# One attention tile for the last 64 queries of both heads, inverse sums written 64-fold, and a plan with new ranks, waits and banks

## The chip, the cores and the metric

The kernel runs on one core of one Trainium2 chip. The metric is the device time of one execution in microseconds (us), the median over several runs. The core's engines work side by side, each on its own queue of instructions in a fixed order, and wait for one another by semaphores: TensorE (PE), VectorE (DVE), ScalarE (ACT), GpSimd (POOL) and SyncE (SP), which here issues the DMA transfers.

## What is computed

Attention with a rotary embedding over 2 batches, 8 heads, 576 positions and 64 channels, then a gated two-layer block without nonlinearity, then eight experts whose weights come from eight rounds of row and column normalisation. The change touches the first part and one product of the second:

```
scores = scale * q_rot @ k_rot.T
scores = scores - max(scores, axis=-1)
attn   = exp(scores)
attn   = attn / (sum(attn, axis=-1) + 1e-09)
x      = attn @ v                       # (1152, 512) after the heads are joined
h      = (x @ w1) * (x @ w2) @ w3
y      = h @ w_out                      # the kernel forms w3 @ w_out first
out    = sum over e of P[:, e] * (relu(y @ moe2_w1[e]) @ moe2_w2[e])
```

## The kernel before

Every float32 product outside the attention weights is split into a high and a low part and made from two or three matmuls. The program has three stages: attention (with the product of w3 and w_out, called w34, beside it), the gated block (`branch`, `merge`), and the experts (`hidden`, `project`). The change lies in the first.

**Tiles.** Two heads form a pair; there are 8 pairs (`NP`). A pair has 576 queries a head, in five query tiles of 128 (`NQ`). The fifth holds 64 queries and 64 columns of zeros (`SPAD` is 640). For each query tile i and head j of pair n: `scores` (L304) makes 128 x 576 scores in PSUM on PE, `row_max` (L329) finds the negated row maximum on DVE, `exponentials` (L333) writes the exponentials and their row sums `sm` on ACT, `transposes` (L348) turns them on PE in three parts a query tile, `moved` (L355) copies each part from PSUM to `et` on ACT or DVE. The tiles form two groups a pair (`TILES`: tiles 0 and 1, tiles 2 to 4). For each group `norm_rows` (L361, L362) adds 1e-9 to the sums on DVE and takes their reciprocals, 4 or 6 numbers a partition; `norm_columns` (L369) spreads each over 64 rows and transposes it by a matmul against the identity; `norm_moved` (L374) copies the result to `r`; `values` (L382) multiplies by v; `x_scale` (L390) multiplies by `r`; `x_hi` and `x_lo` (L401, L405) split the result.

**Conversions.** The weights of the gated block arrive as 64-bit words. One load of 512 KB (`wide`) needs three DVE steps (L183 `low_bits`, L186 `signed`, L191 `joined`), two on ACT (L178, L196) and a subtraction `lo_part` (L199) on POOL or DVE. There are 8 such loads of w_out, 16 of w3, and in the gated block 16 of w1 and w2 (`w12_unit`).

**w34.** `w34_product(u, j)` is three matmuls of 512 columns (L226 to L228). Eight products fill one bank of PSUM, which `w34_hi` (ACT, L233) and `w34_lo` (DVE, L238) then empty. Bank i = 0 to 6 lies in the one-slot pool `psW`; bank 7 (`NEARLY`) is made after the attention stage in the pool `u` of the gated block.

**The order.** A `Plan` sets each engine's order while the program is built. It simulates the engines with a cost for each step and, whenever an engine is free, takes the ready step of lowest rank. `SIGNAL` is what a result costs on the way to another engine; `slots` are the buffers. The steps then stand in this order in the queues; on the chip each engine follows its queue whatever the real durations are. Products of w34 have rank 1000 (L524), so the plan takes one only when PE has nothing else ready. Until the first product, idle time that the plan sees on PE is filled with matmuls of the identity (L541, tile `w`). After the plan come `w12_unit(0)`, the eight products of bank 7, and the branches of the gated block (L140 to L142; their gate product `gf` on DVE is L584).

Of the kernel before, what the change touches and what calls it, by code (L numbers as in the profile page):

```python
# [18 lines left out]
P = 128  # L19
# [20 lines left out]
NEARLY = 7  # L40
NSTEP = 2 * E
# [7 lines left out]
class Plan:  # L49
# [5 lines left out]
    SIGNAL = dict(pe=0.28, act=0.12, dve=0.1, pool=0.12, sp=1.7)  # L55
# [11 lines left out]
    def order(self):  # L67
# [7 lines left out]
        def start(needs, takes, e, ports):  # L75
# [7 lines left out]
            at = [t + (0.0 if by == e else self.SIGNAL[by]) for t, by in map(done.get, needs)]  # L83
# [32 lines left out]
def attention_two_moes(ctx: ExitStack, tc: tile.TileContext, rope, qk, v, mw12, mw3t, mwo, wg, ew1, ew2, out):  # L116
# [20 lines left out]
    def three(ps, terms):  # L137
# [15 lines left out]
    psW, psX, psS, psT = (  # L153
        aps.enter_context(tc.tile_pool(name=n, bufs=k, space=PSUM)) for n, k in (("psW", 1), ("psX", 1), ("psS", 2), ("psT", 2))
# [95 lines left out]
    QK0 = [first[:, o : o + 2 * n].rearrange("p (a s) -> p a s", a=2) for o, n in ((0, SPAD), (2 * SPAD, S))]  # L250
# [52 lines left out]

    def scores(n, i, j):  # L304

        if j == 0:
            st["e", n, i] = att_p.tile([P, 2, S], F32, name="e", bufs=2)
            st["nm", n, i] = att_p.tile([P, 2], F32, name="nm", bufs=4)
            g, k, _ = group(i)
            if k == 0:  # L310
                st["sm", n, g] = att_p.tile([P, 3, 2], F32, name="sm", bufs=3)
        js = half(j)
        if n:
            q, k = SQ[n % 2][:, j], keys(n)
            terms = [(q, k[:, j]), (q, k[:, 2 + j])]
        else:
            (qh, ql), (kh, kl) = ([t[js, x] for x in range(2)] for t in QK0)
            terms = [(qh, kh), (qh, kl), (ql, kh)]
        st["s", n, i, j] = ps = psS.tile([P, 2, 512], F32, name="s")
        for x, (q, k) in enumerate(terms):  # L320
            for h in range(2):
                pe.matmul(  # L322
                    ps[:, h, :HS], q[:, i * P : (i + 1) * P], k[:, h * HS : (h + 1) * HS],
                    start=(x == 0), stop=(x == len(terms) - 1),
                )
# [5 lines left out]
    def exponentials(n, i, j):  # L331
# [3 lines left out]
            AF.Exp, bias=st["nm", n, i][:, j : j + 1], accum_out=st["sm", n, g][:, k, j : j + 1],  # L335
        )

    def transposes(n, i, part):

        rows = min(P, S - i * P)  # L340
        e = st["e", n, i].rearrange("p j r -> p (j r)")
# [589 lines left out]
```

## Time and profile before

| | us |
|---|---|
| median of 3 runs | 1174.78 |
| lowest, highest | 1173.91, 1178.76 |
| the profiled execution | 1180.39 |
| its span | 1178.6 |
| PE busy | 1148.2 (97% of the span) |
| DVE busy | 730.7 (62%) |
| ACT busy | 427.7 (36%) |

The profiled execution is 5.6 us above the median; its rows are used for durations and differences. The shares are means over three stages. The attention stage ends at 212.3 us, the first matmul of the gated block starts at 246.05 us, and from 300 us on PE is busy throughout. In a view by stretches, "busy" counts time in which at least one instruction of the engine is under way; PE's matmuls overlap, so a PE that is busy all the time can still be far from its best rate.

### The profile page before, as it was taken

To read this page: it belongs to the slowest core of one execution; us is meant where nothing else is said; L and a number is where in the kernel's file an instruction comes from. 1 tells how busy PE (TensorE), PEld (TensorE's weight loads), DVE (VectorE), ACT (ScalarE), POOL (GpSimd) and SP (SyncE) were. 2 spreads that over 40 slices of the span, in tenths; PEclk is the share of its full clock that TensorE was granted. 3 is DMA by queue.
4 is the path that set the end of the run, shared out by engine and by line. 5 is a ranking of instruction groups with operands and counts; after the bars stand their busy time and mean duration, and the time that the engine had idled before them with its cause. 6 is when DMAs were issued, how large, how long until landed. Compare 5 with 4: busy or idle time off the path is not lost.

```text
span 1178.6 us, 17761 instructions
## 1 busy us (share of the span) xinstructions
PE 1148.2 (97%) x7087; PEld 1009.4 (86%) x7087; DVE 730.7 (62%) x1347; ACT 427.7 (36%) x903; POOL 203.7 (17%) x205
## 2 busy tenths in 40 slices
PE   8989999889999999999999999999999999999998
PEld 7666677688999888889898898998988989889887
DVE  5788777686443485656566556565565666565643
ACT  3767577344332342323232223223222232222311
POOL 2456451142000000201201011111020120110100
PEclk7999999999999999999999999999999999999999
DMA  6766562343100011211111111111021111110102
GB/s 216 199 182 192 168 181 75 105 148 108 54 19 18 19 37 36 71 37 37 54 36 55 36 36 56 53 36 54 20 71 37 36 55 51 40 54 19 36 9 72
DMA packets 28034, 83.07 MB, mean 70 GB/s; under 512 B 3760, under 2 KB 5296, under 8 KB 27952
## 3 DMA queue, kind: packets, MB, share of 16 engines
q1 hardware_dynamic: 27408, 81.36, 22.1%
q8 instruction: 55, 0.90, 0.3%
q10 hardware_dynamic: 544, 0.59, 0.2%
q14 instruction: 27, 0.22, 0.1%
HBM read 67.19 MB, written 2.36 MB: 59 GB/s over the span
## 4 chain that ended last, share of the span: by engine, by line
PE 87%; DVE 7%; DMA 3%; issue 1%; ACT 1%; POOL 0%; SPq 0%; ACTq 0%; DVEq 0%
PE z L764 11%; PE z L763 11%; PE z L765 11%; PE T L722 4%; PE T L723 4%; PE T L724 4%; PE s L322 3%; PE x L382 3%; PE t L348 3%; PE Q L724 3%; PE Q L722 3%; PE Q L723 3%; PE A L724 3%; PE A L723 3%; PE A L722 3%; PE u L140 3%
## 5 line engine op out<-in xcount | busy, mean ns | idle before, releaser
L765 PE MATMUL z<-w,h 128*128 128x512 f32 x576 | 226.3, 393 | 0.0
L772 DVE SCALAR_TENSOR_TENSOR acc<-z,pr,acc 128x512 f32<-128x512 f32 x135 | 101.0, 748 | 56.7 <-PE z L765 56.6
L765 PEld LDWEIGHTS z<-w,h 128*128 128x128 f32 x576 | 108.0, 187 | 25.3 <-DVE h L729 0.2
L764 PE MATMUL z<-w,y 128*128 128x512 f32 x320 | 126.4, 395 | 0.0
L763 PE MATMUL z<-w,y 128*128 128x512 f32 x320 | 126.4, 395 | 0.0
L642 POOL TENSOR_TENSOR sums<-wide 128x256 f32<-128x256 f32 x28 | 22.9, 818 | 575.3 <-DMA wide<-in_ew_dram 313.6
L764 PE MATMUL z<-w,h 128*128 128x512 f32 x256 | 101.6, 397 | 0.0
L763 PE MATMUL z<-w,h 128*128 128x512 f32 x256 | 100.8, 394 | 0.0
L134 ACT CAST w<-wide 128x768 fp32r<-128x768 f32 (+1 forms) x64 | 60.4, 943 | 93.4 <-PE z L764 65.1
L728 ACT ACTIVATE y<-tmp 128x320 fp32r<-128x320 f32 x96 | 45.2, 470 | 113.8 <-DVE tmp L744 62.3
L728 ACT ACTIVATE h<-tmp 128x256 fp32r<-128x256 f32 x96 | 39.9, 416 | 127.4 <-DVE tmp L744 120.8
L135 DVE TENSOR_TENSOR w<-wide,w 128x768 fp32r<-128x768 f32 (+1 forms) x64 | 69.6, 1088 | 26.5 <-PE T L724 14.8
L140 PE MATMUL u<-x,w 128*128 128x320 f32 (+1 forms) x256 | 76.4, 298 | 3.4 <-DVE gf L584 3.0
L142 PE MATMUL u<-x,w 128*128 128x320 f32 (+1 forms) x256 | 75.7, 296 | 0.0
L141 PE MATMUL u<-x,w 128*128 128x320 f32 (+1 forms) x256 | 75.4, 295 | 0.0
L329 DVE TENSOR_REDUCE nm<-s 128x1 f32<-128x576 f32 x80 | 59.1, 751 | 19.7 <-PE s L322 19.3
L764 PEld LDWEIGHTS z<-w,y 128*128 128x128 f32 x320 | 60.7, 190 | 5.7
L763 PEld LDWEIGHTS z<-w,y 128*128 128x128 f32 x320 | 60.2, 188 | 6.0
L333 ACT ACTIVATE e<-s,nm 128x576 f32<-128x576 f32 x80 | 59.2, 742 | 15.6 <-DVE nm L329 14.2
L729 DVE SCALAR_TENSOR_TENSOR h<-tmp,y 128x320 fp32r<-128x320 f32 x96 | 47.4, 494 | 26.0 <-ACT y L728 25.8
L348 PEld LDWEIGHTS t<-ident,e 128*128 128x128 f32 (+1 forms) x360 | 39.8, 145 | 26.0 <-ACT e L333 9.8
L722 PE MATMUL T<-x,w 128*128 128x320 f32 x192 | 60.0, 312 | 0.1
(205 smaller groups left out, 3040.5 us busy)
## 6 DMA issues: line engine op xcount, KB each, us to landing
wide<-in_ew_dram SPq DMA_DIRECT2D x64, 512.0 KB, 3.5
wide<-in_mw3t_dram SPq DMA_DIRECT2D x16, 512.0 KB, 4.1
wide<-in_mw_dram SPq DMA_DIRECT2D x16, 512.0 KB, 3.5
raw<-in_qk_dram SPq DMA_DIRECT2D x14, 576.0 KB, 4.6
kk<-raw SPq DMA_DIRECT2D x56, 144.0 KB, 3.7
wide<-in_mwo_dram SPq DMA_DIRECT2D x8, 512.0 KB, 4.3
sq<-raw SPq DMA_DIRECT2D x28, 144.0 KB, 3.4
v<-in_v_dram SPq DMA_DIRECT2D x8, 320.0 KB, 3.7
```

The costliest lines, as they stand in the source:

```text
L140: pe.matmul(ps, wh, xh, start=(i == 0), stop=False)
L141: pe.matmul(ps, wh, xl, start=False, stop=False)
L142: pe.matmul(ps, wl, xh, start=False, stop=(i == n - 1))
L348: pe.transpose(ps[:, t, :rows], e[:rows, c : c + P], ident[:rows, :rows])
L722: pe.matmul(ps, h[:, ws], x[0], start=(first and k == 0), stop=False, **kw)
L723: pe.matmul(ps, h[:, ws], x[1], start=False, stop=False, **kw)
L724: pe.matmul(ps, l[:, ws], x[0], start=False, stop=(k == 1), **kw)
L728: act.activation(h, src, AF.Relu)
L763: pe.matmul(ps, hh[:, f, ts], wh, start=(f == 0), stop=False)
L764: pe.matmul(ps, hh[:, f, ts], wl, start=False, stop=False)
L765: pe.matmul(ps, hl[:, f, ts], wh, start=False, stop=(f == FT - 1))
L772: dve.scalar_tensor_tensor(out=acc[t], in0=ps, scalar=p, in1=acc[t], op0=ALU.mult, op1=ALU.add)
```

## The change

Four query tiles of each head stay as they are. The fifth becomes one tile (`MIX`) for both heads: rows 0 to 63 are the last 64 queries of the first head, rows 64 to 127 those of the second. `mixed_scores` accumulates both heads' terms in one PSUM tile, where zeros in the other head's half keep them apart; the second head's keys stand rotated by 64 so that the nine blocks of 128 columns line up, and v is laid out to match. So a pair has 9 score tiles, row maxima and exponentials in place of 10. The query copies for the second head are split in two, so a pair has 6 of these DMAs in place of 4 (7 pairs).

The sums get their 1e-9 on ACT (`norm_sums`). `norm_rows` is now one reciprocal that reads each sum 64 times and writes 256 or 320 numbers a partition; `norm_columns` transposes that.

In the plan: products of w34 have rank 87 + 4u + j in place of 1000 + 4u + j; banks are emptied at rank -200 in place of 42; bank 6 (`LATE`) lies in the pool of the transposes; norms and values come at later ranks; L183 counts as a user of the port that DVE and POOL share; some `SIGNAL` values are larger and PE gets 0.15 more (`SLACK`); the gaps on PE are filled more fully; the PSUM pools are opened in another order.

```diff
-    SIGNAL = dict(pe=0.28, act=0.12, dve=0.1, pool=0.12, sp=1.7)
+    SIGNAL = dict(pe=0.28, act=0.14, dve=0.1, pool=0.12, sp=2.0)
+    SLACK = 0.15
...
+        dst, src = f32(SQ[n % 2][half(x ^ j), j]), raw[n, 0][half(j), 1 - x]
+        if j == 0:
+            sp.dma_start(dst[:, :S], src)
+        else:
+            sp.dma_start(dst[:, : MIX * P], src[:, : MIX * P])
+            sp.dma_start(dst[:, MIX * P + HD :], src[:, MIX * P :])
...
+    def mixed_scores(n):
+        query_tile(n, MIX)
+        st["s", n, MIX, 0] = ps = psS.tile([P, 2, 512], F32, name="s")
+        terms = []
+        for j in range(2):
...
+            pieces = [(0, 0, 0, HS), (1, 0, HS, HS)] if j == 0 else [(0, 0, HD, HS), (1, 0, HD + HS, HS - HD), (1, HS - HD, 0, HD)]
+            terms += [(q, k, pieces) for q, k in new]
...
+    def norm_sums(n, g):
+        sm = st["sm", n, g][:, : 4 + g]
+        act.activation(sm, sm, AF.Copy, bias=1e-9)
     def norm_rows(n, g):
-        dve.tensor_scalar(sm[:, :k], sm[:, :k], 1e-9, None, op0=ALU.add)
-        dve.reciprocal(sm[:, :k], sm[:, :k])
+        st["rb", n, g] = rb = att_p.tile([P, 5, D], F32, name="rb", bufs=2)
+        dve.reciprocal(rb[:, :k], sm.unsqueeze(2).to_broadcast([P, k, D]))
     def norm_columns(n, g):
-        for i in range(len(TILES[g])):
-            for j in range(2):
-                pe.matmul(ps[half(j), i], sm[:, i, j : j + 1].to_broadcast([P, D]), ident, start=True, stop=True)
+        for i in range(2):
+            pe.transpose(ps[:, i], rb[:, 2 * i : 2 * i + 2].rearrange("p j d -> p (j d)"), ident)
...
-            step(norm_rows, a, {"dve": 0.35}, r, needs)
+            step(norm_sums, a, {"act": 0.2}, r, needs)
+            step(norm_rows, a, {"dve": on_dve((4 + g) * D)}, r, [(norm_sums, *a)], [("rb", a)], [("sm", a)])
...
-            ({"dve": 0.37}, (), ["cvu"], [], ()),
+            ({"dve": 0.37}, (), ["cvu"], [], both),
...
+            bank = "psT" if i >= LATE else "psW"
+            place = (psT, "t") if i >= LATE else (psW, "w34")
-                (w34_product, u, j), {"pe": 0.7}, 1000.0 + 4 * u + j, ...
+                (w34_product, u, j), {"pe": 0.7}, 87.0 + 4 * u + j, ...
-            step(w34_hi, (i,), {"act": act_ps(DM)}, 42.0, [(w34_product, u, 3)])
+            step(w34_hi, (i,), {"act": act_ps(DM)}, -200.0, [(w34_product, u, 3)])
...
-                for _ in range(int((at - idle_from - 0.3) * 0.7 / 0.21) if filling else 0):
+                for _ in range(int((at - idle_from - 0.05) / 0.22) if filling else 0):
```

What this does to the order shows at three places. The first is PE's queue at the end of the attention stage, before: the last norm (`sm`), the last values (`x<-et`), then products of w34 (three rows each).

```order
L369 MATMUL t<-ident,sm 64x128 x6
L348 MATMUL t<-ident,e 128x64 x3
L382 MATMUL x<-et_2214,v_95 64x320 x10
L226 MATMUL w_2210<-y 128x512
L227 MATMUL w_2210<-y 128x512
L228 MATMUL w_2210<-y 128x512
L226 MATMUL w_2210<-y 128x512
L227 MATMUL w_2210<-y 128x512
L228 MATMUL w_2210<-y 128x512
```

After the last values 28 products stand here, in four banks, before bank 7 (`u`). The same place after the change:

```order
L363 MATMUL s<-kk,sq_93 128x64
L388 MATMUL t<-ident,e 128x128 x6
L391 MATMUL t<-ident,e 128x128 x4
L394 MATMUL t<-ident,e 64x64 x2
L424 MATMUL t<-ident,rb 128x128 x2
L427 MATMUL t<-ident,rb 64x64 x2
L440 MATMUL x<-et_2393,v_95 64x320 x10
L231 MATMUL u<-y 128x512
L232 MATMUL u<-y 128x512
L233 MATMUL u<-y 128x512
```

Bank 7 now follows the last values directly; the 28 products stand further up, among the attention steps of pairs 3 to 7.

The second place is such a point further up on PE, in pair 7 of the changed kernel, where one bank of w34 (`w_2028`) ends and the next (`w_2184`) begins.

```order
L231 MATMUL w_2028<-y 128x512
L232 MATMUL w_2028<-y 128x512
L233 MATMUL w_2028<-y 128x512
L391 MATMUL t<-ident,e 128x128 x4
L394 MATMUL t<-ident,e 64x64 x2
L340 MATMUL s<-kk,sq_93 128x288 x4
L440 MATMUL x<-et_1902,v_94 64x256 x2
L424 MATMUL t<-ident,rb 128x128 x2
L427 MATMUL t<-ident,rb 64x64 x2
L231 MATMUL w_2184<-y 128x512
```

A handful of attention matmuls stands between the last product of one bank and the first of the next, which waits until ACT and DVE have emptied the bank.

The third place is DVE's queue at the last group of pair 7, before:

```order
L329 TENSOR_REDUCE nm<-s 128x1 x2
L361 TENSOR_SCALAR sm<-sm 128x6
L362 RECIPROCAL sm<-sm 128x6
L355 COPY et_2214<-t 128x3x64
L199 TENSOR_TENSOR y<-cvu,y 128x512
L183 TENSOR_SCALAR cvu<-wide 128x512
L186 SCALAR_TENSOR_TENSOR cvu<-wide,cvu 128x512
L191 SCALAR_TENSOR_TENSOR cvu<-cvy,cvu 128x512
L390 TENSOR_TENSOR xs<-x,r 128x320
L405 TENSOR_TENSOR x<-xs,x 128x320
```

and after:

```order
L370 TENSOR_REDUCE nm<-s 128x1
L407 COPY et_2393<-t 128x3x128
L418 RECIPROCAL rb<-sm 128x320
L407 COPY et_2393<-t 128x3x64
L448 TENSOR_TENSOR xs<-x,r 128x320
L463 TENSOR_TENSOR x<-xs,x 128x320
L188 TENSOR_SCALAR cvu<-wide 128x512
L191 SCALAR_TENSOR_TENSOR cvu<-wide,cvu 128x512
L188 TENSOR_SCALAR cvu<-wide 128x512
L196 SCALAR_TENSOR_TENSOR cvu<-cvy,cvu 128x512
L191 SCALAR_TENSOR_TENSOR cvu<-wide,cvu 128x512
L140 TENSOR_TENSOR wgs<-wgraw,wgs 128x4x8
```

The reciprocal has 320 numbers in place of 6. Before, the conversions shown are of w3, and those of five more loads of w3 and of the two loads of `w12_unit(0)` follow the last `x_lo`. After the change the steps of w3 and of `w12_unit(0)` on DVE all stand above the last `x_lo`, and those shown below it are of `w12_unit(1)`. Ahead of the first `gf` DVE's queue holds the conversion of five w1/w2 loads in both kernels. What is left of `w12_unit(0)` stands on ACT (here the changed kernel, where `w_2498` is its tile and `w_2549` that of unit 1) and, as two `lo_part`, on POOL:

```order
L411 ACTIVATE sm<-sm 128x5
L407 COPY et_2393<-t 128x6x64
L432 COPY r<-t 128x320
L459 CAST x<-xs 128x320
L201 CAST w_2498<-cvu 128x512 x2
```

The two casts of `w_2498` come directly behind the last `x_hi`.

Counted over the plan, DVE has 72 row maxima in place of 80, 16 reciprocals of 256 or 320 numbers in place of 16 small ones with 16 additions, 4 small copies (two of 192, two of 384 numbers) in place of 7, 10 `x_lo` in place of 6 and 9 `lo_part` in place of 8; the fillers on PE are 78 in place of 49, 29 in place of 19 of them ahead of the first scores.

## Rows read from the trace of the kernel before

**Rows 1.** Stretches: length, busy us (instructions) of PE, PEld, DVE, ACT, POOL; clock; DMA.
```profile
0.00:40.00 40.00, 35.64 (x199) 29.42 (x199) 24.42 (x43) 19.23 (x42) 11.51 (x15) 0.83 0.67 205
15.00:20.00 5.00, 5.00 (x19) 4.11 (x20) 3.30 (x4) 3.17 (x7) 0.06 (x1) 0.50 0.82 286
40.00:120.00 80.00, 71.71 (x519) 52.70 (x518) 69.82 (x109) 54.79 (x131) 44.32 (x29) 0.96 0.66 193
120.00:212.30 92.30, 90.31 (x649) 64.75 (x648) 66.61 (x115) 62.59 (x151) 32.48 (x21) 0.98 0.47 133
212.30:235.20 22.90, 18.70 (x79) 14.51 (x80) 15.35 (x25) 8.89 (x16) 3.86 (x3) 1.00 0.36 119
```

**Rows 2.** Timeline of PE, 209 to 247 us: start, us, instruction [idle before <-releaser].
```profile
209.38 2.91 PE L382 MATMUL x<-et,v 128*64 128x320 f32 x20
...
216.65 0.50 PE L226 MATMUL w<-y 128*128 128x512 f32 x1 [1.40 <-DVE keep L238]
...
230.92 0.50 PE L226 MATMUL w<-y 128*128 128x512 f32 x1 [1.40 <-DVE keep L238]
...
238.85 0.50 PE L226 MATMUL u<-y 128*128 128x512 f32 x1 [2.20 <-DVE keep L238]
...
246.05 0.31 PE L140 MATMUL u<-x,w 128*128 128x320 f32 x1
```

**Rows 3.** DVE by line and shape, 0 to 246 us: busy, mean ns | idle before.
```profile
L329 DVE TENSOR_REDUCE nm<-s 128x1 f32<-128x576 f32 x80 | 59.1, 751 | 19.7 <-PE s L322 19.3
...
L355 DVE COPY et<-t 128x384 f32<-128x384 f32 x40 | 21.7, 550 | 12.6 <-PE t L348 12.4
...
L361 DVE TENSOR_SCALAR sm<-sm 128x4 f32<-128x4 f32 x8 | 5.8, 724 | 2.3 <-ACT e L333 2.3
...
L361 DVE TENSOR_SCALAR sm<-sm 128x6 f32<-128x6 f32 x8 | 5.1, 634 | 2.2 <-ACT e L333 2.2
...
L355 DVE COPY et<-t 128x192 f32<-128x192 f32 x7 | 2.3, 338 | 2.4 <-PE t L348 2.4
L362 DVE RECIPROCAL sm<-sm 128x6 f32<-128x6 f32 x8 | 1.5, 192 | 0.3
...
L362 DVE RECIPROCAL sm<-sm 128x4 f32<-128x4 f32 x8 | 1.4, 178 | 0.3
```

**Rows 4.** The same view in the gate rounds of the experts, 405 to 460 us.
```profile
L818 DVE RECIPROCAL rs<-rs 128x9 f32<-128x9 f32 x8 | 1.7, 211 | 0.1
...
L817 DVE TENSOR_SCALAR rs<-rs 128x9 f32<-128x9 f32 x8 | 1.3, 166 | 0.1
```

**Rows 5.** Timeline of POOL and DVE around a late norm, 61 to 65 us.
```profile
61.88 3.01 POOL L265 TENSOR_TENSOR raw<-raw,tab 128x1152 f32<-128x1152 f32 x1 [0.48 <-issue]
...
62.33 2.60 DVE L361 TENSOR_SCALAR sm<-sm 128x6 f32<-128x6 f32 x1
```

**Rows 6.** Timeline of DVE, ACT and POOL after the last values, 212 to 225 us.
```profile
212.44 0.49 DVE L390 TENSOR_TENSOR xs<-x,r 128x320 f32<-128x320 f32 x1 [1.22 <-PE x L382]
213.46 0.49 DVE L405 TENSOR_TENSOR x<-xs,x 128x320 fp32r<-128x320 f32 x1 [0.52 <-ACT x L401]
...
216.65 1.14 DVE L135 TENSOR_TENSOR wgs<-wgraw,wgs 128x32 fp32r<-128x32 f32 x1
217.78 0.43 DVE L183 TENSOR_SCALAR cvu<-wide 128x512 int32<-128x512 int32 x1
218.24 0.69 DVE L186 SCALAR_TENSOR_TENSOR cvu<-wide,cvu 128x512 int32<-128x512 int32 x1
...
219.48 0.62 ACT L196 CAST y<-cvu 128x512 fp32r<-128x512 f32 x1 [2.97 <-PE w L227]
...
223.60 1.29 POOL L199 TENSOR_TENSOR y<-cvu,y 128x512 fp32r<-128x512 f32 x1 [5.86 <-ACT y L196]
```

**Rows 7.** Waits, 246 to 300 us: engine, line <- releaser: us, times, longest.
```profile
PEld u L140 <- DVE gf L584: 4.3, 5, 1.7
```

**Rows 8.** PE by line and shape, 0 to 246 us, columns as in group 3.
```profile
L322 PE MATMUL s<-kk,sq 128*128 128x288 f32 x280 | 54.1, 317 | 0.8 <-DMA sq<-raw 0.8
```

More of the change, by code (lines that the diff above doesn't have):

```diff
@@ L82, in start @@
                 return None
[L83 removed]
+            at = [t + (0.0 if by == e else self.SIGNAL[by] + self.SLACK * (e == "pe")) for t, by in map(done.get, needs)]
             return max([busy[e], port if e in ports else 0.0, *at])
@@ L316, in scores @@
         else:
-            (qh, ql), (kh, kl) = ([t[js, x] for x in range(2)] for t in QK0)
+            (qh, ql), (kh, kl) = ([t[half(j), x] for x in range(2)] for t in QK0)
             terms = [(qh, kh), (qh, kl), (ql, kh)]
@@ L325, in scores @@
                 )
+    def mixed_scores(n):
[3 more added lines that the diff above has]
+        for j in range(2):
+            if n:
+                q, k = SQ[n % 2][:, j, MIX * P :], keys(n)
+                new = [(q, k[:, j]), (q, k[:, 2 + j])]
+            else:
+                (qh, ql), (kh, kl) = ([t[:, x] for x in range(2)] for t in (mix0[:, j], QK0[1]))
+                new = [(qh, kh), (qh, kl), (ql, kh)]
+            pieces = [(0, 0, 0, HS), (1, 0, HS, HS)] if j == 0 else [(0, 0, HD, HS), (1, 0, HD + HS, HS - HD), (1, HS - HD, 0, HD)]
+            terms += [(q, k, pieces) for q, k in new]
+        for x, (q, k, pieces) in enumerate(terms):
+            for h, c, f, w in pieces:
+                pe.matmul(
+                    ps[:, h, c : c + w], q, k[:, f : f + w],
+                    start=(x == 0), stop=(x in (len(terms) // 2 - 1, len(terms) - 1)), skip_group_check=(x >= len(terms) // 2),
+                )
     def row_max(n, i, j):
@@ L345, in transposes @@
         st["t", n, i, part] = ps = psT.tile([P, 4, P], F32, name="t")
-        for t in range(3):
-            c = (3 * part + t) * P
-            pe.transpose(ps[:, t, :rows], e[:rows, c : c + P], ident[:rows, :rows])
+        e = st["e", n, i].rearrange("p j r -> p (j r)")
+        if i < MIX:
+            for t, c in enumerate(((0, 1, 2), (3, 5 + 3, 4), (5, 6, 7))[part]):
+                pe.transpose(ps[:, t], e[:, c * P : (c + 1) * P], ident)
+            return
+        for t in range(3 * part, min(3 * part + 3, MID)):
+            pe.transpose(ps[:, t - 3 * part], e[:, t * P : (t + 1) * P], ident)
@@ L350, in moved @@
+        if part:
+            for j in range(2):
+                pe.matmul(ps[half(j), 1, :HD], e[:, MID * P : S], ident[:, half(j)], start=True, stop=True)
     def moved(n, i, part, eng):
-        rows = min(P, S - i * P)
         g, _, q0 = group(i)
-        dst = st["et", n, g][:, 3 * part : 3 * part + 3, q0 : q0 + rows]
-        src = st["t", n, i, part][:, :3, :rows]
+        et = st["et", n, g]
+        if i < MIX:
+            dst = et[:, (slice(0, 5, 2), slice(6, 9), slice(1, 6, 2))[part], q0 : q0 + P]
+            src = st["t", n, i, part][:, :3]
+        else:
+            b = (slice(0, 6), slice(6, 9))[part]
+            dst = et[:, b, q0 : q0 + HD]
+            src = st["t", n, i, part].rearrange("p t (j q) -> p (t j) q", j=2)[:, : b.stop - b.start]
@@ L371, in norm_moved @@
     def norm_moved(n, g):
-        k = len(TILES[g])
-        st["r", n, g] = r = att_p.tile([P, 3, P], F32, name="r", bufs=2)
-        act.copy(r[:, :k], st["rt", n, g][:, :k])
+        st["r", n, g] = r = att_p.tile([P, G1], F32, name="r", bufs=2)
+        ng = (G0, G1)[g]
+        act.copy(r[:, :ng], st["rt", n, g].rearrange("p i q -> p (i q)")[:, :ng])
     def values(n, g, t):
@@ L459, in attention_two_moes @@
             r = t + i * TILE
-            for j in range(2):
+            for j in range(2 - (i == MIX)):
                 tk = [("psS", (n, i, j))]
```

110 lines of the change are left out of this document (65 added, 45 removed).

## The prediction

> **What bounds the kernel now.** Read first the stretches [rows 1], then PE's timeline where the attention stage ends [rows 2], then DVE's instructions by shape [rows 3, 4]. The stretches show two different kernels in the first 246 us. Up to 212.3 us attention runs, and the engine nearest to its limit from 40 to 120 us is DVE: 69.82 of 80 us, 87.3%. ACT has 54.79 and is not last. PE shows 71.71 there and 90.31 of 92.30 later, but its busy time counts overlapping matmuls and fillers, so it says little about room. From 212.3 us on the picture turns: attention is over, DVE is busy for 15.35 of 22.90 us, and PE works alone through products of w34, each bank waiting for DVE to empty the one before: 1.40 us at the first of the three changes, 1.40 at the third, 2.20 at the last [rows 2]. The first matmul of the gated block starts at 246.05 us, 33.8 us after the last values end (209.38 + 2.91 = 212.29). So the stage has a tail that only PE needs, and in front of it 200 us in which DVE has some idle time left. From 300 us on nothing changes.
>
> **What the change does, part by part.** Let T be the end of the last values, 212.29 now.
>
> *The tail.* Its 28 products go up into the attention stage. Two bank changes lie (230.92 - 216.65) = 14.27 us apart, 7.13 a bank with a wait of 1.40, so eight products cost 5.7 us and 28 cost 20.0. What remains behind T is bank 7, 5.7 us. Beside it run the last `x_scale`, `x_hi` and `x_lo`, which end 1.7 us after T (213.46 + 0.49 - 212.29), then on ACT and POOL the rest of `w12_unit(0)`: a cast of 0.62 and two `lo_part` of 1.29 [rows 6], in all 1.7 + 0.6 + 2.6 = 4.9 us. Bank 7 covers that, with 0.8 to spare; without the cover it costs the difference alone. The branch starts at T + 5.8. DVE still has three of the five conversions ahead of the first `gf` to do after the last `x_lo`, 3 x (0.43 + 0.69 + 0.69) = 5.4 us with 1.14 and 0.69 for two others, T + 9 in all, about when the first `gf` is due. I put that at 1 us more waiting, between 0 and another 4.3 us, what PE waits for `gf` today [rows 7]. The stage therefore ends at T + 6.8 in place of 246.05, and the change pays as long as T stays below 239.
>
> *DVE's work.* Eight row maxima go: 8 x 0.751 = 6.0 us. The sixteen additions and small reciprocals go: 5.8 + 5.1 + 1.5 + 1.4 = 13.8 us [rows 3]. Most of the additions' time is waiting: one took 2.60 us beside a POOL instruction of 3.01 that began just before it [rows 5], while the same operation takes 0.166 undisturbed [rows 4]. Copies: 7 of 192 numbers (2.3 us) become two of 192 and two of 384, 2 x 0.338 + 2 x 0.550 = 1.8 us. Four more `x_lo` at 0.49 [rows 6] are 2.0 us, one more `lo_part`, priced as the other two-input step of 512 numbers (0.69), 0.7 us.
>
> Against this stand 16 reciprocals of 256 or 320 numbers, planned at about 0.4 us. The trace prices them otherwise. With 4, 6 and 9 numbers a reciprocal takes 178, 192 and 211 ns [rows 3, 4], 33 ns for five numbers more, 6.6 ns a number; an addition of 9 takes 166. Carried on (estimates), 256 numbers cost 178 + 252 x 6.6 = 1841 ns and 320 cost 2264: 8 x 1.84 + 8 x 2.26 = 32.8 us. At the low end it streams like the subtraction of 320 numbers at 0.49 us [rows 6]: at most 16 x 0.49 = 7.8 us. At the high end it also waits for POOL as the additions did: their mean excess over 0.166 is 10.9/16 - 0.166 = 0.51 us, 8.2 us more, 41 in all. I take 32.8, since the slope is measured on this very operation.
>
> The Trainium skill, in "VectorE: DVE Perf Modes", section "Walkthrough: the 8-slice pipeline in each mode", says that the reciprocal is an iterative divide with a repeat count of 8, against one result a cycle for an addition. That speaks against the 64-fold form. Eight passes at the page's 0.96 GHz would be 8.3 ns a number, an estimate, and 41 us where the slope of the rows gives 32.8. By it T would come out 9 us later. The trace agrees in kind, at 6.6 ns.
>
> Net for DVE: -6.0 - 13.8 - 0.5 + 2.0 + 0.7 + 32.8 = +15.2 us.
>
> *T.* Up to 212.3 us DVE is busy for 24.42 + 69.82 + 66.61 = 160.9 us [rows 1]. From the tail 15.35 - 0.49 - 0.49 - 1.14 = 13.2 us of conversions and bank emptying move in front of T. The two loads of `w12_unit(0)`, 2 x (0.43 + 0.69 + 0.69) = 3.6 us, also stand above the last `x_lo`, but where the last tile drains and DVE waits; I put them at nothing, at most 3.6. The sum is 160.9 + 13.2 + 15.2 = 189.3 us. The first 40 us, bound by loads and the first pair, keep their 24.4. The rest, 164.9 us, at the best rate that DVE holds over a long stretch (87.3%), takes 188.9 us: T = 229. At 94% T would be 215, at 82% 241; these are the ends.
>
> *PE and its clock.* In the first 40 us the granted clock is 0.83, with 15 to 20 us at 0.50, that is 1.2 of 2.4 GHz, and DVE has 3.30 of 5 us there [rows 1]. Ten more fillers stand ahead of the first scores and close gaps in which PE idles now; later ones cost up to what they delay. I give this -2 us, between 0 and the missing clock of 40 x 0.17 = 6.8. T = 227.
>
> *Without a price.* The scores keep their columns: the joint tile adds a few short matmuls. ACT loses 8 exponentials and gains 16 additions on a handful of numbers; it is not last. Fourteen more small DMAs pass through SP's queue, behind which the later loads stand; PE waits 0.8 us for query copies in the whole run [rows 8], so I price them at nothing, and at 2 us if each pair waited as now once more. The copy of the zeros' tile and the pool order lie in idle time.
>
> *Sum.* The gated block starts at 227 + 6.8 = 233.8 in place of 246.05: 12 us less. Against the profiled execution, 1180.4 - 12 = 1168. The median of the runs shown is 5.6 us below it, and the forecast is for such a median: 1174.8 - 12 = **1163 us**.
>
> **Rivals.** *The reciprocal streams.* Then DVE's net is 15.2 - 25.0 = -9.8 us, and its sum gives 40 + 139.9/0.873 = 200; PE would be last before that, so I take T = 205: branch at 212, 34 us less, 1141. For it: the cost in the plan. Against: the slope in rows 3 and 4.
>
> *DVE fills better than before.* With its waits for POOL gone and conversions spread to the end it reaches 94%: T = 213 with the clock term, branch at 220, 26 us less, 1149. Against: it has held 87.3% at best.
>
> *PE takes DVE's place.* If PE has no room, the 20.0 us of products simply extend attention, and six bank changes inside it, with only a handful of matmuls between, wait 0.5 us each at least and 1.40 as in the tail at most: T = 212.3 + 20 + 3 to 8 = 235 to 240, the branch at about 243, 3 us less, 1172: no change. For it: PE's 90.31 of 92.30 us. Against: overlap and fillers in that figure.
>
> *Slower: queues in order.* DVE's reciprocals stand ahead of row maxima, and PE's first product of a bank stands ahead of scores. Where a reciprocal takes 1.5 us more than planned, the bank is emptied later, PE stops, the next scores come late, and DVE idles. If no added work finds idle time, T = 212.3 + 13.2 + 15.2 + 6 x 1.40 = 249, the branch at 256, 10 us more: 1185. This decides once T passes 239, that is when DVE's rate after 40 us falls below 164.9/199 = 83%. For it: 72% in the stretch from 120 to 212 us, where products stand between attention steps already [rows 1]. Against: conversions were scarce there, so DVE had less to do.
>
> **How the numbers follow.** The forecast has 0.43, streaming 0.10, fuller DVE 0.14, PE 0.16, slower 0.17. What a measurement can tell from no change is about 0.5%, 5.9 us. The forecast's own range is T from 222 to 233, 1157 to 1169, nearly all of it faster (0.39 of 0.43). With streaming and fuller DVE and a little of the PE case (0.03), faster has 0.66. Within 0.5% lie most of the PE case (0.13), 0.04 of the forecast and 0.02 of the slow one, 0.19. Slower has 0.15. The range leaves out most of the streaming case and the end of the slow one: 1146 to 1182.
>
> **What would show it.** In the profile after: reciprocals of 1.8 and 2.3 us, or near 0.45 if they stream; no product of w34 between the last values and bank 7, and a branch some 6 us behind them; DVE at 87% or more from 40 us to the end of attention; T near 227. PE stops of 1 us or more at the first product of a bank, `row_max` waiting for scores for far more than today's 19.3 us in all [rows 3], or a branch that waits for ACT or POOL would each name the step that is wrong. The forecast falls if T lies beyond 239, or if the time beyond the branch's start changes.

## The result and the profile after

The changed kernel takes 1182.1 us (median of 20 runs, 1177.4 to 1185.6); the kernel before, run beside it, 1175.2. The ratio is 1.0051, 95% interval 1.0035 to 1.0067: slower by half a per cent, about 6 us, where 12 us less were forecast. The time lies just beyond the upper end of the range, 1182. The two profiled executions lie 5.2 us (before) and 2.6 us (changed) above these medians, so they differ by 4.4 us only; a T below is that of one execution.

Let T be, as in the prediction, the end of the last values. The stretches of the changed kernel, which answer to [rows 1] and are cut at T = 243.70 and at the first matmul of the gated block, 249.98:

```profile
0.00:40.00 40.00, 36.19 (x261) 30.51 (x262) 31.64 (x46) 22.02 (x52) 13.58 (x18) 1.00 0.69 218
15.00:20.00 5.00, 4.16 (x30) 3.31 (x29) 4.62 (x6) 2.75 (x8) 3.82 (x2) 1.00 0.72 266
40.00:120.00 80.00, 68.42 (x475) 50.10 (x474) 70.27 (x94) 51.11 (x123) 36.98 (x23) 0.96 0.61 186
120.00:243.70 123.70, 111.39 (x685) 80.34 (x684) 91.89 (x132) 69.48 (x166) 40.87 (x26) 0.94 0.47 133
243.70:249.98 6.28, 5.59 (x25) 4.62 (x25) 3.38 (x5) 1.82 (x4) 2.55 (x2) 1.00 0.02 3
```

The tail behind T is 6.28 us in place of 33.8. But T has gone from 212.29 to 243.70, so the gated block starts 3.9 us later than before (246.05, [rows 2]). From there to the end both kernels take the same: 1183.0 - 250.0 = 933.0 us after, 1178.6 - 246.1 = 932.5 before, and all twelve experiments lie between 932.5 and 934.6. Everything happened in the first 250 us.

The end of the attention stage on PE, answering to [rows 2] (start, length, instruction, and in brackets idle time and what ended it):

```profile
235.90 1.12 PE L391 MATMUL t<-ident,e 128*128 128x128 f32 x4 [2.17 <-ACT e L374]
...
238.43 0.66 PE L424 MATMUL t<-ident,rb 128*128 128x128 f32 x2 [0.99 <-DVE rb L418]
...
239.28 4.42 PE L440 MATMUL x<-et,v 128*64 128x320 f32 x20
244.40 0.50 PE L231 MATMUL u<-y 128*128 128x512 f32 x1 [0.69 <-DVE xs L448]
...
249.98 0.31 PE L145 MATMUL u<-x,w 128*128 128x320 f32 x1
```

Bank 7 alone stands between the last values and the gated block, as forecast. DVE by shape up to T, answering to [rows 3] (count | busy, mean ns | idle before):

```profile
L370 DVE TENSOR_REDUCE nm<-s 128x1 f32<-128x576 f32 x72 | 52.3, 745 | 11.8 <-PE s L340 9.6 <-PE s L363 1.9
...
L418 DVE RECIPROCAL rb<-sm 128x320 f32<-128x320 f32 x8 | 17.2, 2147 | 2.5 <-ACT sm L411 2.5
L418 DVE RECIPROCAL rb<-sm 128x256 f32<-128x256 f32 x8 | 14.0, 1747 | 0.7 <-ACT sm L411 0.7
```

The 64-fold reciprocals take 31.2 us. Where the time went is seen in the last two head pairs, up to T. The same columns as in the stretches, first the kernel before, then the changed one with its last 7.7 us:

```profile
166.00:212.29 46.29, 45.77 (x344) 32.66 (x342) 31.07 (x56) 31.86 (x77) 12.21 (x9) 1.00 0.30 87
```

```profile
168.00:243.70 75.70, 67.79 (x409) 48.51 (x408) 52.49 (x77) 40.23 (x94) 18.83 (x12) 0.93 0.36 107
236.00:243.70 7.70, 6.71 (x34) 3.32 (x34) 2.37 (x2) 1.00 (x3) 0.00 (x0) 0.58 0.00 0
```

Up to about 167 us the two kernels keep step: the last norm of pair 5 starts on PE at 166.2 us before and at 167.6 after. Then the two last pairs take 46.3 us before and 75.7 after, 29.4 more. They hold 9 products of w34 before and 32 after (instructions of the first product line in these stretches, without one that begins at T). A product costs 5.7 / 8 = 0.71 us, so 23 more are 16.4 of the 29.4 us. What PE waits for in these pairs, as the list of waits has it (total, times, longest), before in the first fence and after in the second:

```profile
PE t L369 <- DVE et L355: 0.2, 1, 0.2
PE t L348 <- ACT e L333: 0.2, 1, 0.2
```

```profile
PE t L391 <- ACT e L374: 2.2, 1, 2.2
PE s L340 <- ACT e L374: 2.1, 1, 2.1
PE t L388 <- ACT et L407: 1.4, 2, 1.1
PE t L388 <- DVE et L407: 1.2, 2, 0.8
PE t L424 <- DVE rb L418: 1.0, 1, 1.0
```

Before, PE waits 0.4 us in 46; after, 7.9 in 76. So 16.4 us of work and 7.5 us of waits make up 23.9 of the 29.4. Most of the rest can be TensorE's clock, which no run here sets apart. Before, it is 1.00 in this stretch; after, 0.93, so 75.7 x 0.07 = 5.3 us of full clock are missing. It stands at 0.50 (1.2 of 2.4 GHz) from about 198 to 201 us, after PE stops of 0.76 and 1.13 us, and from 236 to 242 us, after the stop of 2.17 us shown above; the last values then take 4.42 us in place of 2.91 [rows 2]. After the stop of 2.13 us that ends at 185.0 it stays at 1.00, so not every stop has this price.

How a wait arises, in the timeline of DVE from 176 us on:

```profile
176.54 1.75 DVE L418 RECIPROCAL rb<-sm 128x256 f32<-128x256 f32 x1 [0.30 <-ACT sm L411]
178.21 0.50 DVE L407 COPY et<-t 128x384 f32<-128x384 f32 x1
178.62 1.74 DVE L204 TENSOR_TENSOR y<-cvu,y 128x512 fp32r<-128x512 f32 x1
180.40 1.54 DVE L188 TENSOR_SCALAR cvu<-wide 128x512 int32<-128x512 int32 x1
181.97 0.69 DVE L191 SCALAR_TENSOR_TENSOR cvu<-wide,cvu 128x512 int32<-128x512 int32 x1
182.70 0.69 DVE L196 SCALAR_TENSOR_TENSOR cvu<-cvy,cvu 128x512 int32<-128x512 int32 x1
183.31 1.42 DVE L370 TENSOR_REDUCE nm<-s 128x1 f32<-128x576 f32 x2
```

The scores of the second of these row maxima were ready at 179.8 + 0.8 = 180.6. DVE, working without a gap, comes to them at 183.3. The exponentials follow at 184.1, and PE, whose next scores need their bank, stands for 2.13 us until 185.0. The reciprocal is only part of what stands ahead of them: L204 and L188 take 1.74 and 1.54 us here, against means of 0.94 and 0.53 up to T.

### The profile page after: what moved, and what is told of

Same layout as the page of the kernel before. It is cut to its first block, busy times and chain, and to the rows that moved or that the text cites. A ratio compares the mean times of both kernels' runs of the same rounds, so it can differ in the third digit from the quotient of the medians.

```text
span 1183.0 us, 17650 instructions
## 1 busy us (share of the span) xinstructions
PE 1144.8 (97%) x7058; PEld 1006.9 (85%) x7058; DVE 742.6 (63%) x1325; ACT 423.0 (36%) x900; POOL 200.8 (17%) x202
## 4 chain that ended last, share of the span: by engine, by line
PE 83%; DVE 9%; DMA 3%; issue 2%; ACT 2%; POOL 1%; SPq 0%; ACTq 0%; DVEq 0%; POOLq 0%
PE z L838 11%; PE z L837 11%; PE z L839 11%; PE T L796 4%; PE T L797 4%; PE T L798 4%; PE Q L798 3%; PE Q L796 3%; PE Q L797 3%; PE A L798 3%; PE A L797 3%; PE A L796 3%; PE u L145 3%; PE u L147 3%; PE u L146 3%; PE x L440 2%
## 5 line engine op out<-in xcount | busy, mean ns | idle before, releaser
L147 PE MATMUL u<-x,w 128*128 128x320 f32 (+1 forms) x256 | 75.7, 296 | 0.0
L374 ACT ACTIVATE e<-s,nm 128x576 f32<-128x576 f32 x72 | 53.3, 742 | 25.8 <-DVE nm L370 25.4
L370 DVE TENSOR_REDUCE nm<-s 128x1 f32<-128x576 f32 x72 | 52.3, 745 | 11.8 <-PE s L340 9.6
L440 PE MATMUL x<-et,v 128*64 128x256 f32 (+1 forms) x320 | 50.9, 438 | 8.7 <-DVE xs L448 8.7
```

Source lines behind the costliest of these rows:

```text
L147: pe.matmul(ps, wl, xh, start=False, stop=(i == n - 1))
L440: pe.matmul(st["x", n, g][half(j), :ng], V[n % 2][:, 2 * t + j], st["et", n, g][:, 2 * t + j * (t < MID)], start=(t == 0), stop=(t == MID),)
```

## The experiments

Three theories stood against each other. **R**: the reciprocals' 31.2 us on DVE hold attention back. **P**: PE is full in the last pairs, so moved products lengthen them whatever DVE does. **O**: the plan prices the reciprocal at 0.4 us, and the order that follows is bad. The table sums up all runs; T, the start of the gated block, DVE's share and TensorE's granted clock come from the one profiled execution, the ratio from all runs beside the kernel before. The code is shortened: a line's old and new form can stand side by side, and `...` marks what is left out.

| kernel | products ahead of T | T, us | gated block, us | DVE busy, 40 us to T | clock, 40 us to T | ratio to before (95%) |
|---|---|---|---|---|---|---|
| before | 28 | 212.3 | 246.1 | 79% | 0.97 | 1 |
| changed | 56 | 243.7 | 250.0 | 80% | 0.95 | 1.0051 (1.0035 to 1.0067) |
| e1 small reciprocal | 56 | 227.2 | 233.5 | 73% | 0.98 | 0.9917 (0.9892 to 0.9941) |
| e2 true price | 56 | 239.2 | 245.5 | 80% | 0.97 | 1.0037 (1.0016 to 1.0057) |
| e3 old ranks | 15 | 199.6 | 243.8 | 83% | 0.97 | 1.0025 (1.0003 to 1.0046) |
| e4 small reciprocal, old ranks | 15 | 196.4 | 240.7 | 72% | 0.98 | 0.9989 (0.9966 to 1.0012) |
| e5 move alone | 56 | 239.2 | 245.5 | 78% | 0.98 | 1.0004 (0.9979 to 1.0028) |
| e6 split reciprocal | 56 | 235.8 | 242.0 | 78% | 0.96 | 0.9991 (0.9968 to 1.0014) |
| e7 small, true price | 56 | 223.0 | 229.3 | 76% | 0.99 | 0.9893 (0.9863 to 0.9923) |
| e8 small, last bank late | 53 | 221.8 | 231.1 | 74% | 0.98 | 0.9918 (0.9887 to 0.9949) |
| e9 both | 53 | 215.8 | 225.1 | 78% | 1.00 | 0.9863 (0.9823 to 0.9902) |
| e10 old fillers | 56 | 245.7 | 251.9 | 80% | 0.96 | 1.0109 (1.0066 to 1.0152) |
| e11 double reciprocal | 56 | 285.6 | 291.9 | 79% | 0.90 | 1.0431 (1.0385 to 1.0476) |
| e12 fillers alone | 28 | 206.4 | 240.0 | 80% | 0.99 | 0.9976 (0.9959 to 0.9994) |

### The reciprocal undone

```
 def norm_rows(n, g):
-    dve.reciprocal(rb[:, :k], sm.unsqueeze(2).to_broadcast([P, k, D]))
+    dve.reciprocal(sm, sm)
 def norm_columns(n, g):
-        pe.transpose(ps[:, i], rb[:, 2 * i : 2 * i + 2]..., ident)
+        pe.matmul(ps[half(j), i], sm[:, m : m + 1].to_broadcast([P, D]), ident, ...)
```

> The changed kernel with one thing undone: the reciprocal is taken of the 4 or 5 sums of a group alone (0.19 us in the rows of before, in place of 1.75 and 2.15), and TensorE spreads it over 64 columns by its small matmuls, as before the change. Ranks, planned costs and the order on every engine stay those of the changed kernel. Theory R (the reciprocals' 31.2 us on VectorE hold attention back): VectorE has 162 - 24 = 138 us to do after the first 40 us, at the same 79.6% T falls from 243.7 to about 213, 1152 us. Theory O (not the work itself, but the order: the plan prices the reciprocal at 0.4 us, and what stands behind it comes late): the stalls go with it, T about 215 to 225, 1154 to 1164. Theory P (TensorE is full in the last pairs, and 28 products more lengthen them whatever VectorE does): T stays at 236 or later, 1175 to 1182 us.

Measured 1167.8 us, 0.9917: 1.3% less than the changed kernel, and less than the kernel before. T is 227.2, between the figures of R and of P. The stretches:

```profile
40.00:227.20 187.20, 174.09 (x1236) 131.37 (x1235) 136.50 (x224) 119.86 (x286) 77.60 (x47) 0.98 0.55 166
227.20:233.50 6.30, 5.61 (x25) 4.62 (x26) 3.41 (x5) 1.82 (x4) 2.54 (x2) 1.00 0.02 3
```

With 25.7 us less to do after the first 40 us (136.50 against 162.15), DVE is busy 73% of the time. Had DVE set the pace, at the 79.6% of the changed kernel T would be 40 + 136.5 / 0.796 = 211, at 87.3% 196. It is 227, so something else holds T there. The reciprocals cost 16.5 us of T on top, not their full length and not nothing: neither R nor P alone. Part of the 16.5 us can be the clock, 0.98 from 40 us to T here and 0.95 in the changed kernel, some 4 and 10 us of full clock missing.

### The price in the plan

```
-step(norm_rows, a, {"dve": on_dve((4 + g) * D)}, ...)
+step(norm_rows, a, {"dve": 0.15 + 0.00625 * (4 + g) * D}, ...)
```

> The changed kernel with the same work, but the plan prices the reciprocal at what it measured, 0.15 + 0.00625 x n us (1.75 and 2.15 in place of 0.36 and 0.43), so the order on the engines fits the real durations. Theory O (the wrong price sets a bad order): T falls from 243.7 to 232 or less, 1171 us or less. Theory R (the work on VectorE) and theory P (TensorE is full): the work is the same, T from 240 to 247, 1178 to 1186 us.

Measured 1181.4 us, 1.0037, an interval that overlaps with that of the changed kernel; T of the profiled execution is 239.2, just below the 240 to 247 of R and P. O, as the main cause, falls: an order that fits the true durations does not bring back more than some 0.4%.

### The move undone, with either reciprocal

e3 takes the changed kernel, e4 takes e1, and both put the old plan of w34 back:

```
-LATE = 6                                 +LATE = 8
-wide_steps(wo_load, ..., 12.0 + 5.9 * j)   +12.0 + 4.5 * j
-wide_steps(w3_load, ..., 50.0 + 4.5 * u)   +48.0 + 4.5 * u
-(w34_product, u, j) 87.0 + 4 * u + j     +1000.0 + 4 * u + j
-w34_hi, w34_lo      -200.0               +42.0
```

> The changed kernel with the old plan for w34: products at rank 1000, in one bank of their own, emptying at rank 42, loads at their old ranks. The joint tile and the 64-fold reciprocal stay. 28 of the 56 products should stand again between the last values and the gated block. Theory R: VectorE has 15 us more to do than in the kernel before, at 87% that is 17 us: T about 229, branch at about 262, 1193 us. Theory P: TensorE sets the pace of the last pairs, so the reciprocals hide, T about 205 to 213, branch at 239 to 247, 1168 to 1176 us. The moved products then cost as much inside attention as behind it.

> Both undone: the joint tile with the small reciprocal and the old plan for w34. Theory R: VectorE has 17 us less than in the kernel before (row maxima, additions and small reciprocals gone, nothing against them), T about 195, branch about 229, 1158 us. Theory P: only what the joint tile takes from TensorE and from the waits counts, T 207 to 212, branch 241 to 246, 1169 to 1175 us.

Measured 1179.9 us (1.0025) and 1176.3 us (0.9989). T comes earlier than expected in three of the four cases and the tail is 10 us longer than in the kernel before, so the times fit neither theory well: e3 lies between the two, e4 above both. But with the old ranks the same reciprocals that cost 16.5 us of T in the changed kernel cost 199.6 - 196.4 = 3.1 us, which R can't explain. (e4 is the joint tile without the 64-fold reciprocal and without the move of w34; the new fillers, `SIGNAL`, `SLACK` and the norms' ranks are still in it.) The stretches after 40 us, e3 first, then e4:

```profile
40.00:199.56 159.56, 147.36 (x1031) 106.78 (x1029) 132.60 (x185) 103.13 (x253) 71.81 (x45) 0.97 0.56 159
199.56:243.78 44.22, 35.15 (x148) 27.17 (x148) 31.04 (x50) 17.65 (x31) 9.75 (x8) 1.00 0.38 127
```

```profile
40.00:196.43 156.43, 145.93 (x1103) 106.40 (x1099) 112.29 (x183) 102.11 (x250) 69.94 (x44) 0.98 0.56 160
196.43:240.72 44.29, 35.18 (x149) 27.17 (x149) 31.09 (x50) 17.61 (x31) 9.77 (x8) 1.00 0.38 127
```

Between e4 and e1 41 products change places (the expectations counted 40; one of the 16 starts right behind the last values), and with them the ranks of the loads and of the emptying, and the conversions that the products need: up to T DVE has 141.8 us of work in e4 and 165.7 in e1. What follows is the price of all that, put on the products. Behind T they cost 44.29 - 6.30 = 38.0 us, 0.93 each, bank waits included. Ahead of T they cost 227.2 - 196.4 = 30.8 us, 0.75 each, where 0.71 is their own time on PE. In this order they found hardly any idle PE to fall into: the move saves the bank waits of the tail and little else. With the 64-fold reciprocals beside them the same 41 cost 243.7 - 199.6 = 44.1 us, 1.08 each, more than the tail did. This is where the gain went.

It also tells why e4 shows no gain, although its T is 15.9 us earlier than before. At rank 1000 a product only fills holes. In e4 15 find one, in the kernel before 28; the 13 others, 0.93 each in the tail, give back 12 of the 15.9 us.

### The move alone

The kernel before with the changes of the plan for w34, the lines above the other way round:

```
-(w34_product, u, j) 1000.0 + 4 * u + j, psW    +87.0 + 4 * u + j, psT if i >= LATE else psW
-w34_hi, w34_lo      42.0                       +-200.0
-wo 12.0 + 4.5 * j, w3 48.0 + 4.5 * u           +wo 12.0 + 5.9 * j, w3 50.0 + 4.5 * u
```

> The kernel before with the new plan for w34 alone: products at rank 87 on, banks 6 and 7 elsewhere as in the changed kernel, emptying at rank -200, loads at their new ranks. Five tiles per head, additions and small reciprocals stay as before. Theory P (TensorE has no room in the last pairs; between the two kernels with the small reciprocal 40 products put T off by 227.2 - 196.4 = 30.8 us, 0.77 each): 28 products put T off by 21.6, T = 234, branch T + 6.3 = 240, 6 us less than before, 1171 us. Theory D (the prediction's: VectorE's work at 87% sets T): T = 227, branch 234, 1163 us. Theory Q (queues: the move alone disturbs them as it does in the changed kernel, where 40 products put T off by 243.7 - 199.6 = 44.1 us, 1.1 each): T = 243, branch 249, 1181 us.

Measured 1176.4 us, 1.0004: no change. T is 239.2, 26.9 us later for 28 products, 0.96 each; 3.5 us of that come from the first pair, whose last norm starts on PE at 44.3 instead of 40.8 in this execution, at a granted clock of 0.70 up to 40 us (before 0.83). Theory D, the prediction's, wanted T = 227 and a gain of 12 us; it fails even without a 64-fold reciprocal in the kernel. The result lies midway between P and Q: the products cost their own time, and some waits beside it.

### Amount or length of the block

```
-dve.reciprocal(rb[:, :k], sm.unsqueeze(2).to_broadcast([P, k, D]))
+dve.reciprocal(rb[:, m], sm[:, m : m + 1].to_broadcast([P, D]))   # one plan step per m
```

> The changed kernel with each 64-fold reciprocal cut into 4 or 5 of 64 numbers (0.15 + 0.4 = 0.55 us each), steps of their own at their real price, so that row maxima may go between them. The same numbers are worked out, with 2 to 3 us more per 16 groups in fixed costs (56 x 0.15 in all, 8 us against 2.4 before). Theory B (blocking: a row maximum that stands behind 2 us of reciprocal is what stops TensorE): the stops shrink, T at 232 or less, 1172 us or less. Theory A (amount: VectorE's 30 us take the room that the waits between the engines need, in whatever pieces): T 239 to 248, 1178 to 1187 us.

Measured 1176.2 us, 0.9991, T = 235.8, between both. Against e2, with the same prices in one piece, it is half a per cent less, and the intervals do not overlap. DVE's line in this kernel, from 40 us on:

```profile
L418 DVE RECIPROCAL rb<-sm 128x64 f32<-128x64 f32 x63 | 29.7, 517 | 2.2 <-ACT sm L411 2.2
```

So cutting the block up, with the freer order that this allows, gives back 0.46 of the 1.20% that lie between e2 and e1, about four tenths. The larger part, 0.7% between e6 and e1, is put down to the amount; that is argued, not tried by itself.

> The changed kernel with every 64-fold reciprocal done twice, to the same place: 31.2 us more for VectorE at the same places of its queue, nothing else. From e1 to the changed kernel 28.2 us of reciprocals put T off by 16.5 us, 0.59 for one. If VectorE is not the limit yet and the price stays: 18 us more, T = 262, 1200 us. If VectorE's 79.6% was all that its waits allow, the price is 1 or more: T = 275 or later, 1213 us or more. If most of the 16.5 us came from the order and not from the amount, the second one costs little: under 8 us, 1190 us or less.

```
-        dve.reciprocal(rb[:, :k], sm.unsqueeze(2).to_broadcast([P, k, D]))
+        for _ in range(2):
+            dve.reciprocal(rb[:, :k], sm.unsqueeze(2).to_broadcast([P, k, D]))
```

Measured 1227.3 us, 1.0431; T = 285.6, 41.9 us later for 31.2 us of DVE work, 1.34 for one: the second case of the expectation. DVE is busy 79% of the time, no more than with single reciprocals, and at that rate 1 us of work would take 1 / 0.79 = 1.27. But the clock differs too: it is 0.90 from 40 us to T in place of 0.95, some 25 us of full clock missing in place of 10, so up to 14 of the 41.9 us can be TensorE running slower between its stops. PE's largest wait from 40 us to T is now:

```profile
PE t L425 <- DVE rb L419: 32.3, 13, 3.8
```

In the changed kernel the same wait has 4.5 us. With e3 and e4 this gives three prices of one us of reciprocal on T: 3.1 / 28.2 = 0.11 with the products outside (e4 to e3), 16.5 / 28.2 = 0.59 with them inside (e1 to the changed kernel), then 1.34. DVE's busy share does not set them by itself: ahead of the added work it is 72, 73 and 80%. What the clock has in each price is not shown.

### The fillers

e10 puts the old rule of the fillers into the changed kernel, e12 the new rule into the kernel before:

```
-for _ in range(int((at - idle_from - 0.3) * 0.7 / 0.21) if filling else 0):
+for _ in range(int((at - idle_from - 0.05) / 0.22) if filling else 0):
```

> The changed kernel with the old rule for the filling matmuls (20 ahead of the first scores in place of 29, and fewer later); all else stays. The prediction gave the new fillers 2 us, between 0 and 6.8. If the clock of the first pair is worth that, the first pair ends 1 to 5 us later than at 36.75 us, and the time is 1 to 5 us longer, 1183 to 1187 us. If what comes early in the first pair is lost again in the waits of the last pairs: the same, 1180 to 1184 us.

> The kernel before with the changed kernel's rule for the filling matmuls (27 ahead of the first scores in place of 19, and more later); all else stays. In e10_old_fillers the old rule made the changed kernel 0.3 to 1% slower against the kernel before than with the new one, a granted clock of 0.981 to 0.988 in place of 0.991 to 0.997. If the fillers buy clock for the first 40 us and this reaches the end: 5 to 8 us less than before, 1168 to 1172 us, granted clock 0.995 or more. If the gap was the changed kernel's own: within 2 us of before, 1174 to 1179 us.

Without the new fillers the changed kernel takes 1190.6 us (1.0109); with them the kernel before takes 1174.9 (0.9976). Both say that the fillers help: 0.24% in the one, 2.9 us with an interval of 0.7 to 4.8; in the other about 0.6%, but with intervals so wide that it may be anything from nothing to 1%. In the first 20 us of e10 (first fence) and of the changed kernel (second):

```profile
5.00:10.00 5.00, 3.88 (x31) 3.52 (x30) 4.09 (x9) 1.30 (x3) 0.00 (x0) 1.00 1.01 365
10.00:15.00 5.00, 3.93 (x22) 2.94 (x21) 4.28 (x9) 3.16 (x8) 0.60 (x1) 0.70 0.67 217
15.00:20.00 5.00, 5.00 (x21) 4.12 (x20) 4.30 (x5) 2.26 (x5) 3.77 (x2) 0.50 0.72 265
```

```profile
5.00:10.00 5.00, 5.00 (x38) 5.00 (x38) 4.36 (x10) 1.30 (x3) 0.00 (x0) 1.00 1.03 374
10.00:15.00 5.00, 5.00 (x42) 4.54 (x41) 4.18 (x9) 3.16 (x8) 0.70 (x1) 1.00 0.65 208
```

With gaps on PE between 5 and 15 us the granted clock falls to 0.50, that is 1.2 of 2.4 GHz; without them it stays at 1.00. The expectation that the gain would be lost in the last pairs did not hold. e10 is even slower than the 1187 us at most that the other one allowed, and e12's 2.9 us lie between its two, 5 to 8 us and within 2.

### A version faster than both

```
-step(norm_rows, a, {"dve": on_dve((4 + g) * D)}, ...)      +{"dve": 0.19}
-step(norm_columns, a, {"pe": (0.24, 0.4)[g]}, ...)         +{"pe": (0.42, 0.63)[g]}
-(w34_product, u, j) 87.0 + 4 * u + j                       +(87.0 if i < LATE else 107.0) + 4 * u + j
```

> The kernel with the small reciprocal and the new plan for w34 (e1_small_reciprocal), planned at real prices: 0.19 us on VectorE, 0.42 and 0.63 us for the spreading on TensorE. As e2_true_price moved nothing measurable, theory: same within 0.4%, 1163 to 1172 us. If the order matters once VectorE has room: 1160 us or less.

> The same kernel (e1_small_reciprocal) with the products of bank 6 ranked 20 later, so that they give way to the last pair's steps and fill what is left of them. In e1 TensorE waits 13.3 us between 40 and 227 us, most of it in the last pairs. If such stops are waits that only lack something to fill them: 4 to 8 us less than e1, 1160 to 1164 us. If the products only move from one place of a full engine to another: the same, 1166 to 1170 us.

> e7_small_true_price and e8_last_banks_late together: small reciprocal, real prices in the plan, bank 6 ranked 20 later. e7 started the gated block at 229.3 us and e8 at 231.1, against 233.5 in e1. If both gains add up: 226 to 227 us, 1160 to 1163 us. If they fill the same gaps of TensorE: 229 us, 1163 to 1166 us.

e7, the first two lines on top of e1, takes 1164.1 us; e8, the third line on top of e1, 1166.2; e9, all of them, 1160.8 us, 1.4% less than the kernel before (0.9863, 0.9823 to 0.9902). e7 or e8 alone cannot be told from e1 by its times, whose intervals overlap, and both lie where "the same" was expected; e9 lies where both gains add up. In the profiled executions the gated block of the three comes 4.2, 2.4 and 8.4 us earlier than in e1. e9 is faster than the kernel before and the changed one beyond doubt. It is the joint tile, the fillers and the moved products, without the 64-fold reciprocal, with real prices in the plan and bank 6 later. Its 38 products more than in e4 put T off by 215.8 - 196.4 = 19.4 us, 0.51 each, less than their own 0.71 on PE: in this order some of them do find room (its prices are not those of e4, though). Its clock is 1.00 from 40 us to T, as in no other kernel here.

## Why the prediction was wrong

**What held.** The tail: the gated block starts 6.28 us behind T (forecast 5.8, and 6.8 with an added wait that did not come: PE's wait for `gf` is 3.7 us, [rows 7] had 4.3 on the weight loads). The price of the reciprocals: 1.75 and 2.15 us, 31.2 in all, against 1.84, 2.26 and 32.8 carried on from 4 to 9 numbers. The sum of DVE's work up to T: 193.8 us (31.64 + 162.15), forecast 189.3. The clock: 2 us forecast, 2.9 measured where the fillers stand alone. The point from which the change pays, T = 239, held among profiled executions: e2, with T = 239.2, has the gated block half a microsecond earlier than before. In the times e2 is 0.4% slower all the same, for the profiled execution of the kernel before lies 5.2 us above its median; measured by medians the point lies some microseconds earlier.

The Trainium skill's "VectorE: DVE Perf Modes", section "Walkthrough: the 8-slice pipeline in each mode", names a repeat count of 8 for the reciprocal. The runs show (2147 - 1747) / 64 = 6.25 ns a number, so in kind it speaks rightly against the 64-fold form, and the size is the measured one. At that page's 0.96 GHz this would be six cycles, an estimate, not eight.

**The step that failed** is "The rest, 164.9 us, at the best rate that DVE holds over a long stretch (87.3%), takes 188.9 us: T = 229". DVE got 79.6%, below the 83% that the prediction itself named as the point where the sign turns. The best stretch was the wrong one to take. Over the whole stage from 40 us to T the kernel before kept DVE busy for 69.82 + 66.61 = 136.4 of 172.3 us [rows 1], 79%; at that rate the prediction's own sum gives 40 + 164.9 / 0.792 = 248, with the clock term 246, and a kernel 7 us slower. That this comes so near to the measured 6 us is in part luck, for in the profiled executions the gated block starts 3.9 us later; the forecast took the median to lie 5.6 us below the profiled execution in both kernels, and in the changed one it is 2.6. Seven other kernels of the table stand at 78 to 80% too, among them the one whose reciprocals are doubled.

Behind it stands a second error, in the first reading. Had DVE been the only bound, e1, with 25.7 us less for it, would have come to 196 or 211; it stopped at 227, with DVE at 73%. PE's 90.31 of 92.30 us [rows 1] was set aside because busy time "counts overlapping matmuls and fillers, so it says little about room". In the last two pairs there are no fillers any more, and the waits of PE, a view that the prediction did not use there, sum to 0.4 us in 46. PE was full exactly where the products went. Priced by PE, a product could only bring the difference between 0.93 us in the tail and 0.75 ahead of it.

T can be read from the table as about the later of two ends: what PE allows (196 with 15 products, 222 to 227 with 53 to 56, taken from e1, e4, e7 and e8 themselves), and 40 us plus DVE's work at about 80%, which gives T within some 4 us in the kernel before, the changed one, e2, e5, e10, e11 and e12. It misses e3 (206 against 199.6), e6 (231 against 235.8) and e9, whose T of 215.8 lies 6 us ahead of e8's with the same 53 products: what PE allows also hangs on the order and the clock. That is a reading which fits eleven kernels of fourteen, not a mechanism that was shown.

The clock term looked at the first 40 us alone. There the fillers brought what it said, but from 40 us to T the clock of the changed kernel is 0.95 where the kernel before has 0.97, some 10 us of full clock missing in place of 5; the prediction had put nothing there.

**The rivals.** "PE takes DVE's place" had the mechanism that the move alone bears out: it gave T = 235 to 240 and no change in time, and the move alone (e5) gave 239.2 and 1.0004. Its extra was looked for at the wrong place, though: bank changes, put at 3 to 8 us, are 0.9 us of waiting in the changed kernel from 40 us to T (PE's waits for `keep` at `w`). It also left out the reciprocals. "Slower: queues in order" had the right sign and, at T = 249 and 1185 us, was the nearest in time; it was reached by adding all of DVE's work to T, of which only part is borne out. Its wrong order by the plan's price is worth little (e2), its row maximum behind a reciprocal at most some four tenths of the reciprocals' cost (e6). "The reciprocal streams" and "DVE fills better" are both refuted by the reciprocal's rows and by 79.6%.

**The sum as the runs have it**, in the profiled executions: from 212.3 the fillers take T to 206.4 (e12; in the times they bring 2.9 us, not 5.9). The 28 products, at 0.84 each in e5 once the slow first pair is taken out (23.4 us), put it to about 230. The joint tile with the small reciprocal brings it to 227.2 (e1), which is a difference of two other figures and was not measured by itself with the new ranks. The 64-fold reciprocals add 16.5: 243.7. The tail gives back 27.5. In the times: the move is worth nothing by itself (e5); fillers, joint tile, move and the plan's other new values together 0.8% (e1); and the reciprocals cost 1.3%, more than all the rest brings.

**What stays open**: why DVE stops at about 80% in kernels with such different orders, and why e3 alone holds 83%; how much of the reciprocals' price is DVE's time and how much the clock that falls with PE's stops; and what `SIGNAL`, `SLACK`, the norms' later ranks, the split copies and the pool order do, none of which was tried by itself. The size of the fillers' gain in the changed kernel is not settled either, and the reciprocals on another engine were not tried.

## What to carry to other kernels

Before work is moved from behind a stage into it, add up what the engine that must do it waits for in the stretch where it will land: if that is near nothing, expect the work to cost about its full time there, so that only the waits that it leaves behind are gained; here it cost 0.75 to 0.84 us a product for 0.71 of work, and 0.51 only after the order was repaired (e9). For another engine, take the rate that it kept over the whole stage (79%), not over its best stretch (87%): in the sum that alone turns the sign here. Look at the clock of the stage as well as at the waits: here a stop of 2.17 us was followed by some 6 us at 0.50. And an operation whose time grows with every number (6.25 ns) belongs ahead of a broadcast, not behind it.

## What the runs showed of the hardware that was not expected

The reciprocal on DVE is nearly linear over the whole span, 6.2 to 6.6 ns a number: 517 ns for 64 numbers, 1747 for 256, 2147 for 320 on each partition, and 178 to 211 ns for 4 to 9 [rows 3, 4]. The run-to-run spread of the kernel before goes with PE's clock: beside e12, runs at a mean granted clock of 0.988 took 1178.8 to 1181.7 us, those at 0.995 to 0.997 took 1170.7 to 1174.9 us. With eight more fillers ahead of the first scores and others after them, all twelve runs were granted 0.994 to 0.999 and took 1173.3 to 1177.1 us: not faster than the best runs without them, but none above 1177.1.
